# A transformer block on one core: one more iota at the end of GpSimd's queue

## The chip, the cores and the metric

The kernel runs on one core of a Trainium2 chip. Its time is the device time of one execution in microseconds (us). A time given for a kernel is the median of several runs. Executions of the same program follow each other on the core.

## The reference

The input x has 2048 rows of 512 numbers in bf16. It is layer-normalised to xn, and three things are added: x itself, an attention block on xn (32 heads of 16 columns each, softmax over all 2048 keys, output projection) and a gated feed-forward block on xn (inner width 1792). Cut to what matters:

```python
def _A_ref(x, wqkv, wo):
    qkv = (x @ wqkv).reshape(B, S, 3, H, Dh)  # then q, k, v by head
    scores = jnp.einsum("bhqd,bhkd->bhqk", q, k) * (Dh ** -0.5)
    p = _softmax(scores, axis=-1)
    o = jnp.einsum("bhqk,bhkd->bhqd", p, v)
    return o.transpose(0, 2, 1, 3).reshape(B, S, D) @ wo

def _B_ref(x, W_gate, W_up, W_down):
    gate = jnp.einsum("bsd,df->bsf", x, W_gate)
    up = jnp.einsum("bsd,df->bsf", x, W_up)
    gate = gate * (gate > 0)
    return jnp.einsum("bsf,fd->bsd", gate * up, W_down)

xn = _layernorm(x, axis=-1)
return x + _A_ref(xn, A_wqkv, A_wo) + _B_ref(xn, B_W_gate, B_W_up, B_W_down)
```

## The kernel before

**The order of the work.** The program is written as a list of operations (`G.op(engine, duration, function, ...)`). A planner in the class `Graph` places them on five queues by dependence, priority and the durations that it is given, and works out the waits between the queues. Each queue then runs strictly in order on its engine: an instruction that waits holds up all that stand behind it on that engine.

**The start.** Four tiles of x (128 rows each) are fetched first (line 723, on SP's queue), then the first columns of Wq and Wk (lines 736 and 737), four more tiles of x, Wv, and the last eight tiles of x, which go to the buffer `hT`. TensorE runs ten matmuls on zeros (`heat`, line 1021) whose result nobody uses. Each of the first tiles is normalised by itself: VectorE takes its mean and variance (lines 810 and 812), for tile 3 ScalarE takes them (lines 801 and 802); VectorE adds the small constant (`vare`, lines 792 and 804); GpSimd raises to the power of -0.5 (`rstd`, lines 794 and 808); VectorE applies it (`xn_sb`, line 833). TensorE transposes the tile (line 858), ScalarE copies it out of PSUM (`xnT`, line 866), and TensorE projects the first keys and queries from it (line 1039). ScalarE and VectorE write the queries of four heads apart, each multiplied with a column of `hmask` that is not zero in the rows of its head alone (lines 1064 and 1065).

**Where the mask comes from.** `hmask` is made from the number of the partition. GpSimd writes that number into `pid`, two columns of the buffer `ints`, with an iota (line 687). It is the first operation of the kernel on GpSimd's queue. VectorE masks it (line 688, `ints`) and compares it four times (line 691, `hmask`). These five instructions stand on VectorE's queue ahead of the first statistics of line 810.

**The long middle.** Scores of 128 keys by 512 queries are made on TensorE (line 138 is the helper that records nearly all matmuls). Most are exponentiated on ScalarE (line 1525, 708 times). For the rest VectorE makes three shifted integer patterns that together stand for the exponential: line 1481 the first, and for most of these the second and third are made by GpSimd with a 64-bit integer addition (line 1495, 308 times). Between these TensorE works off the projections and the feed-forward block as fillers.

**GpSimd's libraries.** The names of the program tell two kinds of operations on GpSimd: those called `stock` (the powers) and the 64-bit addition. `load_library` (line 883) places one 64-bit addition of two words at line 886, ordered behind all operations called `stock`, and gives the planner 7000 ns (`LIB_NS`) for it. The compiler puts a pair of instructions `MODIFY_POOL_CONFIG` on GpSimd's queue wherever the next operation is of the other kind, and ahead of the first one of the program: so a pair stands in front of the iota of line 687 and one in front of the addition of line 886. The last operation on GpSimd's queue is an addition of line 1495.

**The end.** Behind the last scores, VectorE and TensorE normalise and project the last heads (`normalise_last`, lines 1272 to 1298), and four tiles of the result are stored, the last by ScalarE's queue (line 1305). At line 584 all queues meet.

Of the kernel before, what the change touches and what calls it, by code (L numbers as in the profile page):

```python
# [83 lines left out]
LIB_NS = 7000  # L84
# [521 lines left out]
def bass_parallel_sum__mha_block__glu_gated_reglu__prompt_kernel(  # L606
# [13 lines left out]
    with ExitStack() as es:  # L620
        def sb(name, shape, dt):
# [4 lines left out]
        pid, word = ints[:, 0:2], ints[:, 2:4]  # L626
# [36 lines left out]
        G = Graph()  # L663
# [17 lines left out]
        t_id, t_pid, t_expo, t_warm, t_zero = (Tile() for _ in range(5))  # L681
        t_masks = [Tile() for _ in range(4)]
# [6 lines left out]
             reads=[t_pid], writes=[t_pid], prio=-890)  # L689
        for v in (0, 2, 1, 3):  # L690
            G.op("DVE", 100, lambda e, v=v: e.tensor_scalar(hmask[:, v:v + 1], pid[:, 0:1], 16.0 * v, QSCALE, op0=ALU.is_equal, op1=ALU.mult),
                 reads=[t_pid], writes=[t_masks[v]], prio=-889 + v)
# [3 lines left out]
                                                    base=0, pattern=[[-1, 128]], channel_multiplier=1),  # L696
             reads=[t_id], writes=[t_id], prio=-898)
        t_rbz = Tile()
# [70 lines left out]
        for j in range(4):  # L769
            for ee in range(2):  # L770
                r0 = 32 * j + DH * ee
                dma(lambda e, r0=r0, ee=ee: e.dma_start(Wo_l[r0:r0 + DH, ee, :], A_wo[D - 128 + r0:D - 128 + r0 + DH, :]), 16,
                    reads=[t_woz], writes=[Tile()], prio=60, after=100)
# [230 lines left out]
        NU = len(units)  # L1004
# [52 lines left out]
        for v in (0, 2, 1, 3):  # L1057
# [3 lines left out]
            for n, (tile, bank, c, x) in enumerate(((pb, 3, slice(0, 384), slice(0, 384)), (bq, 1, slice(128, 256), slice(384, 512)))):  # L1061
# [4 lines left out]
                     reads=[tile, t_masks[v]], writes=[] if n else [t1], joins=[q0], prio=MASK_LATE + v if late else -787 + 0.2 * v + 0.1 * n,  # L1066
# [446 lines left out]
        for u, unit in enumerate(units):  # L1513
# [8 lines left out]
            for sub in range(2):  # L1522
# [3 lines left out]
                              reads=[ts], writes=[tr], prio=u - 100, order=[exp_ops[u - 1]] if u else [], name="ex%d" % u)  # L1526
# [7 lines left out]

        assert li == len(plan)

        normalise_last(*last_pv)

        def blank_early(e):
# [38 lines left out]
```

## Time and profile before

| what | value |
|---|---|
| time, median of 3 runs | 692.18 us (691.84 to 692.42) |
| time of the profiled execution | 691.33 us |
| its span, first to last instruction | 689.4 us |
| TensorE busy (matmuls) | 673.2 us, 98% of the span |
| ScalarE busy | 659.8 us, 96% |
| VectorE busy | 588.5 us, 85% |
| GpSimd busy | 330.0 us, 48% |
| mean granted TensorE clock | 0.992 |

PE is TensorE's matmuls, PEld its weight loads, DVE VectorE, ACT ScalarE, POOL GpSimd, SP the queue that issues most DMAs. A name with a q behind it (POOLq, SPq) is the sequencer of that engine: instructions that compute nothing. In a row of the timeline stand the start, the time taken, the engine, the line, the operation with its output and input, and in square brackets how long the engine had been idle and what ended that. The chain that ended last is followed back from the last instruction, at each step to what released it. "issue" is time in which the engine waited for nothing that the profile shows. A row of the windows gives, for a stretch of time, the busy time of each engine with the number of its instructions, the granted TensorE clock (1.00 is full speed) and the busy share of the DMA engines.

### The profile page before, as it was taken

Reading aid. Unit: us, or ns where it says so; the run is one execution under the profiler, and the core shown is the slowest. Engines: PE = TensorE matmul, PEld = TensorE weight load, DVE = VectorE, ACT = ScalarE, POOL = GpSimd, SP = SyncE. Lnnn points to the kernel's source line nnn. Section 1 sums busy time; section 2 is a strip of 40 time slices with the busy share of each in tenths; the row PEclk is TensorE's granted clock in tenths of the full one; section 3 lists DMA queues with packets and bytes.
Section 4 is the critical chain, followed back from the end, with each engine's and each line's share of the span. In section 5 each row is a group of like instructions: output and inputs, shape, how many; then the busy total and the mean of one; then the engine's idle time right before and its main releaser. Section 6 shows DMA issues by size and latency. Waiting matters only on the chain.

```text
span 689.4 us, 46060 instructions
## 1 busy us (share of the span) xinstructions
PE 673.2 (98%) x22320; PEld 399.4 (58%) x20890; DVE 588.5 (85%) x993; ACT 659.8 (96%) x725; POOL 330.0 (48%) x340
## 2 busy tenths in 40 slices
PE   5899999999999999999999999999999999999997
PEld 2455665566655556656565556555655667655574
DVE  5975897999989878889899787889999887998876
ACT  3999999999999999999999999999999999999984
POOL 2311334445455546545455564445566654555540
PEclk7999999999999999999999999999999999999999
DMA  6330010231311111110101121110100121120001
GB/s 190 60 70 27 21 44 12 53 93 36 92 42 27 44 49 38 31 41 11 45 6 28 32 50 47 30 42 16 39 5 18 39 69 41 42 58 13 20 13 34
DMA packets 51478, 28.77 MB, mean 42 GB/s; under 512 B 18840, under 2 KB 50328, under 8 KB 51288
## 3 DMA queue, kind: packets, MB, share of 16 engines
q1 hardware_dynamic: 51144, 25.70, 14.4%
q8 instruction: 169, 2.77, 1.8%
q14 instruction: 21, 0.17, 0.1%
q10 hardware_dynamic: 144, 0.13, 0.1%
HBM read 18.22 MB, written 2.10 MB: 29 GB/s over the span
## 4 chain that ended last, share of the span: by engine, by line
PE 82%; ACT 12%; DVE 4%; issue 2%; POOL 0%; DVEq 0%; POOLq 0%
PE ps L138 81%; ACT ring L1525 12%; DVE stats L810 1%; DVE qd L1481 1%; PE ps L1039 1%; PE ps L858 0%; DVE qd L1498 0%; DVE xn_sb L1298 0%; POOL rstd L794 0%; DVE v_aug L978 0%; DVE kT L971 0%; DVE xnT L878 0%; DVE ints L688 0%; DVE qT L1065 0%; DVE up_sb L1277 0%
## 5 line engine op out<-in xcount | busy, mean ns | idle before, releaser
L1525 ACT ACTIVATE ring<-ps 128x1024 bf16<-128x1024 f32 x708 | 651.7, 1115 | 8.2 <-PE ps L138 8.1
L138 PE MATMUL ps<-qT,kT 64*32 64x512 bf16 x8192 | 463.8, 375 | 1.7 <-issue 0.6
L1495 POOL INT64_ADD qd<-qd x308 | 317.2, 1040 | 309.5 <-DVE qd L1481 176.7
L1481 DVE TENSOR_SCALAR qd<-ps 128x512 int16<-128x512 f32 x632 | 413.3, 685 | 59.4 <-PE ps L138 53.1
L138 PE MATMUL ps<-qd,v_aug 64*32 64x512 bf16 x3792 | 301.4, 375 | 0.2
L138 PE MATMUL ps<-ring,v_aug 64*32 64x512 bf16 x2832 | 241.9, 375 | 0.6 <-issue 0.5
L1461 PEld LDWEIGHTS <-kT 64*32 64x32 bf16 x8132 | 175.1, 92 | 110.9 <-issue 25.1
L1433 PEld LDWEIGHTS <-v_aug 64*32 64x32 bf16 x5252 | 128.2, 92 | 64.1 <-issue 11.2
L138 PE MATMUL ps<-xnT,wgs 64*32 64x512 bf16 x1792 | 137.5, 375 | 0.0
L138 PE MATMUL ps<-xnT,wus 64*32 64x512 bf16 x1792 | 135.8, 375 | 0.0
L138 PE MATMUL ps<-Wd,hT 64*32 64x512 bf16 x768 | 58.4, 375 | 0.2 <-issue 0.2
L913 PEld LDWEIGHTS <-wgs 64*32 64x32 bf16 x1792 | 43.8, 92 | 23.4 <-issue 4.1
L913 PEld LDWEIGHTS <-hT 64*32 64x32 bf16 x1792 | 43.7, 92 | 22.6 <-issue 2.4
L913 PEld LDWEIGHTS <-wus 64*32 64x32 bf16 x1792 | 44.5, 92 | 21.2 <-issue 2.7
L1130 DVE COPY up_sb<-ps 128x512 f32<-128x512 f32 x56 | 38.4, 685 | 7.4 <-PE ps L138 7.3
L1134 DVE SCALAR_TENSOR_TENSOR hT<-ps,up_sb 128x512 bf16<-128x512 f32 x56 | 38.3, 684 | 2.7 <-PE ps L138 2.6
L138 PE MATMUL ps<-Wv,hT 64*32 64x512 bf16 x512 | 39.4, 375 | 0.2 <-issue 0.2
L138 PE MATMUL ps<-Wk,hT 64*32 64x512 bf16 x512 | 39.2, 376 | 0.0
L138 PE MATMUL ps<-Wo_p,x_sb 64*32 64x512 bf16 x480 | 37.1, 376 | 0.1
L138 PE MATMUL ps<-xnT,Wq 64*32 64x512 bf16 x480 | 37.2, 375 | 0.0
L138 PE MATMUL ps<-xnT,Wk 64*32 64x512 bf16 x480 | 36.1, 375 | 0.7 <-issue 0.4
L138 PE MATMUL ps<-Wv,xnT 64*32 64x512 bf16 x512 | 30.7, 375 | 0.3
(82 smaller groups left out, 224.8 us busy)
## 6 DMA issues: line engine op xcount, KB each, us to landing
wus<-in_B_W_up_dram SPq DMA_DIRECT2D x38, 128.0 KB, 2.4
wgs<-in_B_W_gate_dram SPq DMA_DIRECT2D x38, 128.0 KB, 2.5
xr_sb<-in_A_x_dram SPq DMA_DIRECT2D x16, 128.0 KB, 2.5
qT<-qf SPq DMA_DIRECT2D x120, 16.0 KB, 2.4
o_sb<-o_sb SPq DMA_DIRECT2D x60, 32.0 KB, 2.5
out_dram<-xn_sb SPq DMA_DIRECT2D x15, 128.0 KB, 1.9
x_sb<-in_A_x_dram SPq DMA_DIRECT2D x8, 128.0 KB, 2.9
Wd<-in_B_W_down_dram SPq DMA_DIRECT2D x6, 128.0 KB, 2.6
```

The lines of the kernel that those rows point to most:

```text
L138: return e.add_instruction(mybir.InstMatmult(name=e.bass.get_next_instruction_name(), engine=mybir.EngineType.PE, ins=[e.lower_ap(x), e.lo ...
L810: G.op("DVE", 580, lambda e, m=m: e.bn_stats(stats[:, m, :], xs(m)), reads=[t_xm[m]], writes=[t_st], prio=pr, order=last_xn if m == 4 and ...
L913: e.ldweights(w()[rows, 32 * j:32 * j + 32], tile_position=(rows.start, 32 * j))
L1039: ins = e.matmul(ps[32 * j:32 * j + 32, BANK[bank], c], w[:, dt, 32 * j:32 * j + 32], xnT[:, dt, x], start=(dt == 0), stop=(dt == DT - 1), ...
L1130: G.op("DVE", 603, lambda e: e.tensor_copy(up_sb[:, tup.slot, :], bank_of(tu)), reads=[tu], writes=[tup], prio=-590)
L1134: G.op("DVE", 603, lambda e: e.scalar_tensor_tensor(out=hT[:, th.slot, :], in0=bank_of(tg), scalar=0.0, in1=up_sb[:, tup.slot, :], op0=ALU ...
L1433: e.ldweights(vs(j), tile_position=(64 * half, 32 * j))
L1461: e.ldweights(ks(m), tile_position=(64 * half, 32 * m))
L1481: G.op("DVE", 601, lambda e, j=j, tx=tx: e.tensor_scalar(qd[:, tq.slot, 512 * j:512 * j + 512], ps[:, BANK[tx.slot], :], IBIAS[3], 0.0, op ...
L1495: G.op("POOL", POOL_NS, lambda e, x=x, n=n: e.int64_add(x().bitcast(I64), raw().bitcast(I64), SHIFTS[n + 1] * LANES), reads=[ti, tq, t_lib ...
L1525: exp_ops[u] = G.op("ACT", 904, lambda e, tr=tr, k0=k0: e.activation(ring[:, tr.slot, :, :], ps[:, 4 * k0:4 * k0 + 2, :], ACTF.Exp, scale= ...
```

## The change

Behind the last addition of line 1495, one more iota is placed on GpSimd's queue. It writes the number of the partition into `pid` again, as line 687 does. Nothing reads it. `order` holds it behind all operations named `p3`, which are the additions of line 1495, and behind the two memsets of `rb`. It has no semaphore to signal. As it is an operation of the first kind behind one of the second, the compiler puts a pair of `MODIFY_POOL_CONFIG` in front of it. As built, GpSimd's queue is longer by these instructions at its end, and every other queue has the same instructions in the same order as before.

```diff
         assert li == len(plan)
 
+        added = [o for o in G.ops if o.name == "p3"]
+        G.op("POOL", LIB_NS, lambda e: e.iota(pid, pattern=[[0, 2]], base=0, channel_multiplier=1), reads=t_masks, writes=[t_pid], prio=NU, order=added + t_rbz.w, name="stock")
+
         normalise_last(*last_pv)
```

## The prediction

> **What bounds the kernel now.** I read the page first (engines, chain), then the chain of the first 20 us in order of time, then the rows around the two places where GpSimd changes its kind of operation, and last the end of GpSimd's queue.
>
> ```profile
> span 689.4 us, 46060 instructions
> PE 673.2 (98%) x22320; PEld 399.4 (58%) x20890; DVE 588.5 (85%) x993; ACT 659.8 (96%) x725; POOL 330.0 (48%) x340
> PE 82%; ACT 12%; DVE 4%; issue 2%; POOL 0%; DVEq 0%; POOLq 0%
> 60.00:100.00 40.00, 39.78 (x1356) 25.87 (x1308) 32.64 (x53) 39.72 (x45) 13.25 (x13) 1.00 0.13 32
> ```
>
> The middle is TensorE with ScalarE close behind: from 60 to 100 us they are busy 39.78 and 39.72 of 40 us (first two engines after the length are PE and PEld, then DVE, ACT, POOL). No wait is left there to shorten. So whatever shifts the start of this stage shifts the end by the same amount, and the change touches only GpSimd's end and, if anything, GpSimd's start.
>
> The chain of the start, from the view of the chain in order of time (start, length, what):
>
> ```profile
> 0.81 0.01 POOLq L687
> 0.82 0.02 issue
> 0.85 0.01 POOLq L687
> 0.86 7.24 issue
> 8.10 0.14 POOL ints L687
> 8.24 0.02 issue
> 8.26 1.17 DVE ints L688
> 9.44 0.02 issue
> 9.46 0.34 DVE hmask L691 x4
> 9.80 0.61 DVE stats L810
> ```
>
> The chain runs through 7.24 us in which GpSimd does nothing that is recorded, between the pair in front of the iota and the iota. VectorE's line 688 waits for the iota, and the first statistics stand behind it.
>
> ```profile
> L687 POOLq MODIFY_POOL_CONFIG  x2: 11/11/11, 0.8 to 0.8; - x2
> L886 POOLq MODIFY_POOL_CONFIG  x2: 11/11/11, 34.6 to 34.6; - x2
> 40.72 0.18 POOL L886 INT64_ADD ints<-ints  x1 [6.32 <-issue]
> 34.40:40.72 6.32, 6.22 (x200) 4.00 (x192) 6.32 (x14) 6.32 (x8) 0.00 (x0) 1.00 0.36 80
> 669.67 1.04 POOL L1495 INT64_ADD qd<-qd  x1 [0.46 <-PE ps L138]
> 670.71:689.40 18.69, 15.20 (x458) 9.07 (x398) 13.23 (x27) 8.83 (x12) 0.00 (x0) 0.97 0.10 32
> ```
>
> The same gap follows the second pair: 6.1 us from 34.6 to 40.72. So the pair itself takes 11 ns twice, and the first operation of the new kind comes 6 to 7 us later: code is exchanged. The second exchange costs nobody anything: in its window PE, DVE and ACT are busy (6.22, 6.32, 6.32 of 6.32 us; I read the columns as above). The last addition of line 1495 ends at 670.71. From there GpSimd is empty for 18.69 us.
>
> What is known of the exchange is also in the Trainium skill (GPSIMD Engine Reference, section 2.1 Instruction dispatch): `ModifyPoolConfig` loads code, and the first call to a freshly loaded kernel pays about 6 us with no visible instruction. The 7.24 and 6.1 us here agree.
>
> **The change, part by part.** *The tail.* It adds a pair, an exchange and an iota behind 670.71. By the rows of the two exchanges this takes 6.1 to 7.24 us, plus 0.14 us for the iota: done at 677.0 to 678.1, some 11 us ahead of the end. What hides it is the 18.69 us of the last window; without that cover it would cost its whole length. No instruction stands behind it on GpSimd but the meeting of all queues at line 584, and nobody waits for `pid`. In the exchange at 34.6 no engine lost time, so I put the tail at 0.
>
> *The start.* I take it that executions follow each other with nothing of GpSimd's between them. Then an execution of before begins with the code of the 64-bit addition in place, since an addition was the last thing that GpSimd did. The pair of line 687 then really exchanges code. An execution of after begins with the code that the iota needs already there. What a pair costs that asks for code already in place, no row shows. It is bounded below by its own two records, 0.02 us, and above by 7.24 us. I take the lower end: each of the gaps in the trace stands where the kind does change, the 308 additions behind line 886 run one after another without such a gap, and the length of the gap fits moving code, which is not needed then.
>
> What the start is then bound by, from the timeline and the tile's view:
>
> ```profile
> 0.74 1.82 SPq L723 DMA_DIRECT2D x_sb<-in_A_x_dram  x4
> DMA to landing us min/median/max: 2.2/2.9/3.5
> 4.78 0.63 ACT L801 ACTIVATE up_sb<-x_sb 128x512 bf16<-128x512 bf16 x1 [2.54 <-DMA x_sb<-in_A_x_dram]
> 6.17 0.19 ACT L802 ACTIVATION_READ_ACCUMULATOR up_sb<-x_sb,warm 128x1 f32 x1
> 9.71 0.68 DVE L810 BATCH_NORM_STATS2 stats<-x_sb 128x6 f32<-128x512 bf16 x1
> 13.03 0.15 DVE L804 TENSOR_SCALAR vare<-warm 128x1 f32<-128x1 f32 x1
> 3.08 0.51 SPq L737 DMA_DIRECT2D Wk<-in_A_wqkv_dram  x1
> Wk<-in_A_wqkv_dram SPq DMA_DIRECT2D x1, 128.0 KB, 3.8
> 14.23 0.62 PE L1039 MATMUL ps<-xnT,Wk 128*32 128x128 bf16 x16
> ```
>
> The iota comes at about 0.9, ends at 1.0; line 688 takes 1.17, line 691 0.34: VectorE is free at 2.6. The first statistics need tile 0 of x. Issued at 0.74 and landing 2.2 to 3.5 later, it is there between 2.9 and 4.2. ScalarE starts on the fourth tile at 4.78 when its DMA lands, the issues are 1.82/4 = 0.46 apart, so tile 0 is there at about 4.78 - 3 x 0.46 = 3.4; I take 3.5. The statistics move from 9.71 to 3.5: **6.2 us**. They are late next for the DMA, no more for the iota, and a pair that cost up to 0.9 us would still be hidden. The others follow: the constant for tile 3 (line 804) moves from 13.03 to 6.8 and needs line 802, done at 6.36; Wk is there at 3.08 + 3.8 = 6.9 and wanted at 14.23 - 6.2 = 8.0. So this term is 5.5 (tile 0 at 4.2) to 6.7 (line 804 on line 802).
>
> *TensorE's clock at the start.* A second gain hangs on the first.
>
> ```profile
> 5.43 0.40 PE L1540 MATMUL ps<-Wo_l 128*128 128x512 bf16 x1
> 12.56 1.74 PE L858 MATMUL ps<-ident,xn_sb 128*128 128x128 bf16 x12 [6.73 <-DVE vare L792]
> 8.50:9.00 0.50, 0.00 (x0) 0.87 0.81 260
> 12.56:18.12 5.56, 5.55 (x79) 0.50 0.27 87
> 19.00:19.20 0.20, 0.20 (x12) 0.73 0.00 0
> 13.20 1.73 ACT L866 ACTIVATE xnT<-ps 128x512 bf16<-128x512 bf16 x3 [6.85 <-PE ps L858]
> 18.80 2.85 ACT L1525 ACTIVATE ring<-ps 128x1024 bf16<-128x1024 f32 x3 [0.39 <-PE ps L138]
> 19.21 0.56 DVE L1079 CAST kT<-ps 128x384 bf16<-128x384 f32 x1 [1.25 <-PE ps L1039]
> ```
>
> The matmuls on zeros end at 5.83. TensorE then stands idle for 6.73 us, the clock falls to half at 8.87 (the window to 9.00 has 0.87), 3.0 us into the idle time, and stays there to 19.1, so that the first transposes and projections, 5.55 us busy, run at half speed. With the first transposes at 12.56 - 6.2 = 6.4 the idle time is 0.5 us. I take it that the clock then does not fall. At full speed 5.55 becomes 2.8 us. Not all of that is gained, as ScalarE's copies of line 866 and VectorE's work lie between: VectorE's one idle stretch there, 1.25 us at line 1079, waits for TensorE and would go. I take **1.2 us**, with 0 (the clock stays at half) and 1.4 us (half of TensorE's 2.8 us, the rest behind ScalarE) as ends. The Trainium skill (TensorE: Matmul & The Clock Gate, Part 1) says that the clock falls after an idle window of about 3.4 us; the 3.0 us here agree within the window's phase, and by that rule too an idle time of 0.5 us leaves the clock as it is.
>
> *What could take it back.* Later loads have room:
>
> ```profile
> 6.08 1.53 SPq L723 DMA_DIRECT2D hT<-in_A_x_dram  x3
> hT<-in_A_x_dram SPq DMA_DIRECT2D x2, 256.0 KB, 5.9
> 22.03 0.69 DVE L810 BATCH_NORM_STATS2 stats<-hT 128x6 f32<-128x512 bf16 x1
> ```
>
> The ninth tile of x is there at 6.08 + 5.9 = 12.0, wanted at 22.03 - 7.4 = 14.6. Everything that SP issues behind 20 us waits for other engines and moves with them.
>
> **The sum.** 691.33 (the profiled execution, span 689.4 and 1.93 around it) - 6.2 - 1.2 + 0 = 683.9 us. The median is 0.85 above that execution (692.18), so for the median 684.8 us. The ends are 692.18 - 8.1 = 684.1 and 692.18 - 5.5 = 686.7. I widen them by 1.3 us on either side: below because a shift of this start may let other small waits before 28 us go, above because the pair may cost some of its 7.24 us also with the code in place (a pair of 3.5 us would bring VectorE to line 810 at 0.86 + 3.5 + 0.14 + 1.17 + 0.34 = 6.0 and leave 3.7 us and half of the clock's term).
>
> **The rivals.** *The pair always loads.* If the pair fetches the code whether or not it is there, the start stays as it is, 0.86 to 8.10, and the tail is hidden: 692.2 us, no change. For it speaks that the program asks for the load with the same instructions in each case, and that no row shows a shorter one; against it only that the trace's loads all do change the code. It would come out the same if something between two executions put other code in place. By the Trainium skill's rule (GPSIMD Engine Reference, section 2.1) that the first call to a freshly loaded kernel pays, it would come out so if a repeated request counts as a fresh load. No row of before can tell.
>
> *The pair costs a part.* Between the two, some 4 to 6 us of the 7.24 remain: VectorE reaches line 810 at 0.86 + 4 + 1.65 = 6.5 to 8.5, a gain of 3.2 to 1.2 us: about 690 us. For it speaks that two instructions are issued, of which one may drop the old code and the other fetch the new; against it that their own records are 11 ns each.
>
> *The tail is seen.* Slower, if the exchange at the end took longer than the 18.69 us from 670.71 to the end: GpSimd would then be the last at line 584. At 20 us it would give 692.2 + 1.3 = 693.5, with no gain at the start. Against it: the two exchanges measured take 6.1 and 7.24 us, the shorter with the DMA engines busy 0.36 of the time, and in the last window they are busy 0.10.
>
> **How the numbers follow.** The forecast (code in place, load skipped) has 0.82, the part 0.05, the load that always runs 0.10, the seen tail 0.03. Differences under 0.2% (1.4 us) can't be told from none here. Faster by more: 0.82 and the part, 0.87. Same 0.10, slower 0.03. The range of the forecast, 682.8 to 688.0, holds nearly all of its 0.82, which leaves out no more than 2 in 10.
>
> **What the profile of after would show.** If right: the iota of line 687 at about 1 us with "issue" before it nearly gone, the first row of line 810 at 3.4 to 4.2 released by a DMA of x, a granted clock that stays up from 6 us on, line 1525 starting near 11.4 in place of 18.80, and at the end an iota at 677 to 678 with nobody waiting. If wrong: the iota of line 687 still at 8.1, or, for the tail, a chain whose last piece is on GpSimd. The second term fails by itself if the first transposes come at 6.4 but windows up to 12 us show 0.50.

## The result and the profile after

| | before | after |
|---|---|---|
| time, median | 692.25 us (4 runs, 691.84 to 692.42) | 683.12 us (4 runs, 681.67 to 683.50) |
| time of the profiled execution | 691.33 us | 682.77 us |
| span | 689.4 us | 680.6 us |
| mean granted TensorE clock | 0.992 | 1.000 |

The ratio is 0.9865 (95% interval 0.9848 to 0.9882): 9.1 us faster. The forecast was 684.8 us with a range of 682.8 to 688.0.

The start of the changed kernel, first by the instructions of line 687 and then by the timeline:

```profile
L687 POOLq MODIFY_POOL_CONFIG  x2: 11/11/11, 1.0 to 1.0; - x2
L687 POOL IOTA ints<- x1: 129/129/129, 1.1 to 1.1; 128x2 int32 x1
```

```profile
1.07 0.13 POOL L687 IOTA ints<- 128x2 int32 x1 [0.64 <-POOLq L1566]
1.23 0.17 DVE L688 TENSOR_SCALAR ints<-ints 128x2 int32<-128x2 int32 x1
1.44 0.34 DVE L691 TENSOR_SCALAR hmask<-ints 128x1 f32<-128x1 int32 x4
2.88 0.69 DVE L810 BATCH_NORM_STATS2 stats<-x_sb 128x6 f32<-128x512 bf16 x1 [1.11 <-DMA x_sb<-in_A_x_dram]
5.84 1.43 PE L858 MATMUL ps<-ident,xn_sb 128*128 128x128 bf16 x12
6.22 0.14 DVE L804 TENSOR_SCALAR vare<-warm 128x1 f32<-128x1 f32 x1
7.96 1.17 PE L1039 MATMUL ps<-xnT,Wq 128*32 128x384 bf16 x32
10.29 3.07 ACT L1525 ACTIVATE ring<-ps 128x1024 bf16<-128x1024 f32 x3
```

The pair is still there and its two records are as long as before, 11 ns each. But the iota follows it at once, at 1.07 us where it stood at 8.10. The mask is ready before the first tile of x, and VectorE's first statistics now wait for the DMA (the square brackets of the fourth row), as forecast. They begin at 2.88 in place of 9.71. ScalarE's first exponential stands at 10.29 in place of 18.80.

The end, by GpSimd's timeline and the windows (after the length: PE, PEld, DVE, ACT, POOL busy, granted clock, DMA share, GB/s):

```profile
660.85 1.04 POOL L1495 INT64_ADD qd<-qd  x1 [0.46 <-PE ps L138]
668.95 0.13 POOL L1538 IOTA ints<- 128x2 int32 x1 [7.05 <-issue]
```

```profile
5.86:12.00 6.14, 5.06 (x109) 2.63 (x107) 5.85 (x22) 5.51 (x12) 2.71 (x5) 1.00 0.94 286
661.89:680.60 18.71, 15.25 (x458) 8.21 (x398) 13.23 (x27) 8.83 (x12) 0.13 (x2) 1.00 0.10 33
```

The exchange at the end takes 7.05 us and lies beside 18.7 us of other work: VectorE and ScalarE are busy in the last window for as long as they were before (13.23 and 8.83 us). TensorE's clock, 0.50 between 9 and 19 us before, is 1.00 in the first of the two windows, and the 32 projections of the queries (line 1039 with Wq) take 1.17 us. Before, the timeline had for them:

```profile
15.32 1.90 PE L1039 MATMUL ps<-xnT,Wq 128*32 128x384 bf16 x32
```

Where do the 9.1 us come from? The first of the 15 rows of VectorE's line 955 serves as a mark: it stands where the start is over and the steady middle begins. Before and after:

```profile
42.91 0.69 DVE L955 TENSOR_SCALAR qf<-ps 128x512 bf16<-128x512 f32 x1 [0.31 <-PE ps L138]
```

```profile
34.62 0.69 DVE L955 TENSOR_SCALAR qf<-ps 128x512 bf16<-128x512 f32 x1 [0.32 <-PE ps L138]
```

The mark is 8.29 us earlier. From the mark to the end the two profiled executions take 646.5 and 646.0 us. So all of the gain that can be placed lies in the start. The half microsecond behind the mark is not explained by the change: in two more profiled executions of the changed kernel, further down, the same stretch took 649.4 and 644.1 us.

### The profile page after: what moved, and what is told of

The parts are those of the page before. It is cut to its first block, busy times and chain, and to the rows that moved or that the text cites. A ratio compares the mean times of both kernels' runs of the same rounds, so it can differ in the third digit from the quotient of the medians.

```text
span 680.6 us, 46065 instructions
## 1 busy us (share of the span) xinstructions
PE 671.9 (99%) x22322; PEld 397.0 (58%) x20890; DVE 587.0 (86%) x993; ACT 659.8 (97%) x725; POOL 330.8 (49%) x341
## 3 DMA queue, kind: packets, MB, share of 16 engines
q8 instruction: 169, 2.77, 1.7%
## 4 chain that ended last, share of the span: by engine, by line
PE 85%; ACT 10%; DVE 4%; issue 0%; DMA 0%; POOL 0%; DVEq 0%
PE ps L138 85%; ACT ring L1525 10%; DVE stats L810 1%; DMA x_sb<-in_A_x_dram 0%; DVE qd L1481 0%; DVE xn_sb L833 0%; DVE qd L1498 0%; DVE mv L812 0%; DVE xn_sb L1298 0%; POOL rstd L794 0%; DVE v_aug L978 0%; DVE kT L971 0%; DVE xnT L878 0%; DVE qT L1065 0%; DVE up_sb L1277 0%
```

## The experiments

They ran in three groups, each on one chip, and each is compared with the kernel before in its own group, whose median was 688.41 us in the first, 692.63 in the second and 687.66 in the third. Absolute times are not compared across groups. The mark (first row of line 955) stood at 34.62, 34.67 and 34.65 us in three profiled executions of the changed kernel, on different occasions, and carries the finer readings.

**A memset in the iota's place.** It computes on GpSimd as well, but needs no exchange, so no pair stands before it.

```diff
-        G.op("POOL", LIB_NS, lambda e: e.iota(pid, pattern=[[0, 2]], base=0, channel_multiplier=1), reads=t_masks, ...
+        G.op("POOL", 100, lambda e: e.memset(pid, 0), reads=t_masks, ...
```

> The changed kernel with a memset of pid in the iota's place. A memset needs no exchange of code, so no pair stands in front of it. Theory (the time depends on which code GpSimd holds when an execution begins): the 64-bit addition's code is left in place, the iota of line 687 comes at 8.1 us as before, 692.2 us. Rival (any further instruction behind the last addition does it): 683.1 us.

Measured: 688.47 us against 688.41, ratio 0.9998 (0.9988 to 1.0008). No gain. The iota of line 687 is back at 7.88 us:

```profile
0.85 7.03 issue
7.88 0.14 POOL ints L687
```

(The chain in order of time.) A further instruction at the end is not what does it.

**Both exchanges at the end.** One 64-bit addition behind the new iota, so that the last code in place is the addition's.

```diff
         G.op("POOL", LIB_NS, lambda e: e.iota(pid, ...), ..., name="stock")
+        G.op("POOL", LIB_NS, lambda e: e.int64_add(word.bitcast(I64), word.bitcast(I64), 0), reads=[t_word], writes=[t_word], prio=NU, order=G.ops[-1:])
```

> The changed kernel with one 64-bit addition of the two words behind the new iota, so that a second pair and a second exchange follow at the end and the addition's code is the last. Theory: the tail takes some 7 + 6 = 13 us, still hidden, but line 687 pays its 7.2 us again: 692.2 us. Rival (the iota or the exchange at the end does it, whatever is left in place): 683.1 us.

Measured: 688.09 us against 688.41, ratio 0.9997 (0.9985 to 1.0008). GpSimd's timeline of the end and of the start:

```profile
667.37 1.04 POOL L1495 INT64_ADD qd<-qd  x1 [0.46 <-PE ps L138]
675.45 0.13 POOL L1538 IOTA ints<- 128x2 int32 x1 [7.04 <-issue]
681.55 0.18 POOL L1539 INT64_ADD ints<-ints  x1 [5.98 <-issue]
```

```profile
8.60 0.13 POOL L687 IOTA ints<- 128x2 int32 x1 [8.18 <-issue]
```

The new iota is there with its exchange, and a second exchange of 5.98 us behind it, both hidden. The start pays again. So neither the iota nor its exchange is worth anything by itself; what counts is the code that an execution leaves in place for the next. This shows at the same time that the code stays in place from one execution to the next. What a first execution finds, behind another program, was not run.

**The clock without the iota.** The kernel before with more matmuls on zeros.

```diff
-            for _ in range(10):
+            for _ in range(38):
```

> The kernel before with 38 in place of 10 matmuls on zeros in line 1021, so that TensorE works until about 12 us and its clock does not fall; the iota still comes at 8.1 us. This is the clock's part alone. Theory: the clock's part is 1.2 to 1.8 us: 690.4 to 691.0 us, the first row of line 810 still at 9.7 us. Rival (the clock gives nothing, and all 9.1 us come from the earlier iota): 692.2 us.

Measured: 687.48 us against 688.41, ratio 0.9982 (0.9971 to 0.9993), by the interval 0.5 to 2.0 us faster. The iota and the statistics stand as in the run with the memset (7.89 and 9.51 us here; 7.88 and 9.50 there). TensorE's clock stays up: the first 12 transposes take 1.41 us, where they took 1.74 before and 1.43 in the changed kernel. The mark moves from 42.30 (the run with the memset) to 41.23, so by 1.07 us:

```profile
41.23 0.69 DVE L955 TENSOR_SCALAR qf<-ps 128x512 bf16<-128x512 f32 x1 [0.32 <-PE ps L138]
```

```profile
42.30 0.69 DVE L955 TENSOR_SCALAR qf<-ps 128x512 bf16<-128x512 f32 x1 [0.32 <-PE ps L138]
```

The first fence is the run with 38 matmuls, the second that with the memset. Against the run with the memset, the clock is worth 1.07 us by itself; against the kernel before it is more, as the section on the prediction shows.

**The iota without the clock.** The changed kernel with a single matmul on zeros.

```diff
-            for _ in range(10):
+            for _ in range(1):
```

> The changed kernel with 1 in place of 10 matmuls on zeros in line 1021: the earlier iota without the warm clock. Theory: the statistics still begin at 2.9 us, the clock is at half for the first projections, and the 1.2 to 1.8 us are lost: 684.3 to 684.9 us. Rival (the clock gives nothing): 683.1 us.

Measured: 681.41 us, ratio to before 0.9897 (0.9874 to 0.9920), 7.0 us faster. The changed kernel was not timed in this group; where it was, its ratios were 0.9865, 0.9896 and 0.9893, with intervals that overlap this one, so the times cannot separate the two. The mark can:

```profile
35.78 0.69 DVE L955 TENSOR_SCALAR qf<-ps 128x512 bf16<-128x512 f32 x1 [0.31 <-PE ps L138]
```

It is 1.16 us later than in the changed kernel's 34.62, in line with the 1.07 us of the run before. The chain shows what is slow:

```profile
6.43 1.11 PE ps L858 x8
7.54 0.55 PE ps L1039 x16
8.09 0.54 PE ps L858 x4
8.63 2.79 PE ps L1039 x43
```

These lengths are those of the kernel before at half clock, whose chain has for the last of these rows:

```profile
15.39 2.79 PE ps L1039 x44
```

The column of the granted clock shows 1.00 in all windows of this run up to 14 us, which the lengths contradict. Where the column and the lengths differ, I go by the lengths (the last section says where the column misleads).

**VectorE's queue alone.** The kernel before with the five instructions of the mask moved behind the statistics of tiles 0 to 2.

```diff
         G.run()
+        q = G.queue["DVE"]
+        masks = [o for o in q if -890 <= o.prio <= -886]
+        third = [o for o in q if o.dur == 580][2]
+        q[:] = [o for o in q if o not in masks]
+        put = q.index(third) + 3
+        q[put:put] = masks
```

> The kernel before with VectorE's five instructions for the mask (lines 688 and 691) moved behind the statistics of tiles 0 to 2 on its queue. Nothing else moves. Theory: the statistics begin at 2.9 us, but the powers of line 794 stand behind the iota on GpSimd and still come at 9.7 us in place of 11.33: 1.7 us faster than before, and the clock still falls. Rival (holding up VectorE's queue was the whole cost of the late iota): 6 us or more faster.

Measured: 691.09 us against 692.63, ratio 0.9972 (0.9957 to 0.9988): 1.5 us between the medians, 0.8 to 3.0 us by the interval. From VectorE's and GpSimd's timeline and the chain:

```profile
2.77 0.69 DVE L810 BATCH_NORM_STATS2 stats<-x_sb 128x6 f32<-128x512 bf16 x1 [1.63 <-DMA x_sb<-in_A_x_dram]
8.19 1.16 DVE L688 TENSOR_SCALAR ints<-ints 128x2 int32<-128x2 int32 x1 [2.50 <-POOL ints L687]
10.18 0.41 DVE L833 TENSOR_SCALAR xn_sb<-x_sb,mv,rstd 128x512 bf16<-128x512 bf16 x1 [0.46 <-POOL rstd L794]
```

```profile
8.03 0.13 POOL ints L687
9.28 0.28 POOL ident L695
9.56 0.59 POOL rstd L794
```

The statistics run at 2.77, but the first power comes at 9.56 all the same, behind the exchange and GpSimd's other work. It is 1.77 us earlier than before (11.33), as expected. The mark stands at 40.26, 2.65 us earlier than before, as the clock also came back sooner (at 15.4 us in place of 19.1). Of the 8.29 us, freeing VectorE's queue alone recovers these 2.65; the other 5.6 were held by GpSimd's own queue.

**Requests for code in place.** The changed kernel with a request for the addition's code in front of ten additions.

```diff
+                    again = n == 0 and nq[0] % 15 == 0
-                    G.op("POOL", POOL_NS, lambda e, x=x, n=n: e.int64_add(...),
+                    G.op("POOL", POOL_NS, lambda e, x=x, n=n, again=again: (e.load_library(library_config.all_libraries[1]) if again else None, e.int64_add(...))[1],
```

> The changed kernel with a further request for the code of the 64-bit addition in front of about ten of the additions of line 1495, while that code is in place. Theory (a request for code in place costs next to nothing): no gap of more than 0.1 us behind any of them that the waits don't explain, time of the changed kernel within 1 us. Rival (only the first request of an execution is skipped): 6 us of GpSimd's time at each, which its idle time hides only in part; later additions are late, several us slower.

Measured: 685.21 us; the changed kernel in the same group 685.25 (its expectation below). The instructions of the line of the additions:

```profile
L1496 POOLq MODIFY_POOL_CONFIG  x20: 11/11/11, 121.2 to 635.5; - x20
L1496 POOL INT64_ADD qd<-qd x308: 1033/1038/1062, 56.9 to 662.5; - x154
...
  issue: 0.2, 1
```

Ten more pairs, and GpSimd's idle time that nothing else explains is 0.2 us in all. One exchange would have been 6. Nor did a wait hide one: in the trace each of the ten additions begins 0.07 to 0.08 us behind its pair. This was the price that no row of before showed: a request for code in place is close to nothing, here at the start and at ten places between 121 and 636 us.

> The changed kernel once more, timed beside the runs below. Theory: 8.3 to 9.3 us under the kernel before; by the starts of one row of TensorE in the traces so far (45.80 us before, 37.50 us after) 8.3 us.

Measured: 685.25 us against 692.63, ratio 0.9896 (0.9880 to 0.9912), 7.4 us faster; mark at 34.67. The expectation of 8.3 to 9.3 was missed; only the upper end of the interval, 8.3 us, reaches it. The start is as early as in the first trace, so the difference lies behind the mark, where this execution took 649.4 us.

**The end without cover.** Two attempts. In the first the new iota waits for VectorE's last instruction:

```diff
+        for o in [o for o in G.ops if o.eng == "DVE"][-1:]:
+            G.ops[-1].deps[o] = True
```

> The changed kernel with the new iota held until VectorE's last instruction (line 1298) is done, so that the exchange of code at the end has nothing beside it. Theory: VectorE ends at 677.4 us of the changed kernel's 680.6; the pair, some 7.05 us and the iota of 0.13 follow: the end comes at 684.7, 4.1 us later than in the changed kernel, and the start stays early. Rival (the exchange runs behind the end of an execution at no cost): same as the changed kernel.

Measured: 683.72 us, ratio to before 0.9880 (0.9855 to 0.9906), the same as the changed kernel in this group (685.25, ratio 0.9896). The instructions of the new line, and GpSimd's timeline:

```profile
L1542 POOLq MODIFY_POOL_CONFIG  x2: 11/11/11, 662.9 to 663.0; - x2
```

```profile
679.09 0.14 POOL L1542 IOTA ints<- 128x2 int32 x1 [16.15 <-DVE xn_sb L1298]
```

The run did not test what it was meant to. The wait belongs to the iota, the pair stands ahead of it, and the exchange began at 663.0 while the iota waited: the iota starts at 679.09, 0.09 us behind the end of VectorE's last instruction at 679.00, with no 7 us between. So an exchange starts when the queue reaches the pair, and hides behind a wait of the instruction that needs it. For the second attempt a memset, which needs no exchange, takes the wait, and the pair and the iota stand behind it:

```diff
+        G.op("POOL", 100, lambda e: e.memset(pid, 0), reads=t_masks, writes=[t_pid], prio=NU, order=added + t_rbz.w)
+        for o in ends:
+            G.ops[-1].deps[o] = True
+        G.op("POOL", LIB_NS, lambda e: e.iota(pid, ...), writes=[t_pid], prio=NU, name="stock")
```

> The changed kernel with a memset of pid, which needs no exchange, waiting for VectorE's last instruction (line 1298), and the pair and the iota behind it. Now the pair itself is held, where in the run before only the iota was. Theory: the exchange has nothing beside it; 6.8 to 7.5 us and the iota follow VectorE's end, which is 3.2 us ahead of the span's end, so the end comes some 4.1 us later than in the changed kernel. Rival (the exchange costs nothing at the end even so): same as the changed kernel.

> The changed kernel, timed beside the held pair on the same chip. Theory: 7 to 9 us under the kernel before, by the trace's start 8.3 us.

Measured: 685.68 us (ratio 0.9970, 0.9959 to 0.9980) with the pair held, 680.70 (0.9893, 0.9872 to 0.9914) for the changed kernel beside it, 687.66 for the kernel before. The changed kernel's 7.0 us are at the lower end of what was expected (7 to 9). Held, the exchange costs 5.0 us of the 7.0 us gained. From the instructions of line 584, where the queues meet, and GpSimd's timeline, of the run with the pair held:

```profile
L584 SPq DRAIN  x1: 13/13/13, 677.8 to 677.8; - x1
L584 POOLq EVENT_SEMAPHORE  x2: 17/17/17, 682.8 to 682.9; - x2
```

```profile
675.44 0.10 POOL L1542 MEMSET ints<- 128x2 int32 x1 [16.12 <-DVE xn_sb L1298]
682.54 0.13 POOL L1545 IOTA ints<- 128x2 int32 x1 [6.99 <-issue]
```

SP, otherwise the last, is done at 677.8; GpSimd comes 5.0 us later. That is the price of the tail without the cover that it has in the changed kernel. It was expected at 4.1 us, and most of the difference comes from a misreading: the expectation put VectorE's end at 677.4 us in the changed kernel, but the three rows of line 1298 end at 678.0, 2.6 us ahead of the span's end in place of 3.2.

## Why the prediction was right, step by step

*The mechanism* was right: the program's last use of GpSimd decides which code the next execution finds, and a request for code in place does not load it. The prediction could only assume both. The run with both exchanges shows the first, the ten requests show the second, and the trace of after shows the two together. Of the rivals, the pair that always loads and the pair that costs a part fall with the iota at 1.07 us; the tail that is seen falls with the iota at 668.95, 11.7 us ahead of the end. The lower end chosen for the unknown price, 0.02 us, was the right one: the iota follows the second record of the pair within 0.1 us. It was a choice: as the prediction says, no row of before could decide it.

*The tail at 0* was right: its length was forecast at 6.1 to 7.24 us plus the iota, measured 7.05 plus 0.13. The run with the pair held puts the cost without cover at 5.0 us.

*The first term* was 6.2 us for the statistics (5.5 to 6.7), measured 6.83 (9.71 to 2.88), just above its own upper end. The step that was off is the arrival of tile 0, taken at 3.5 us from the spacing of the issues; it was there at 2.88, slightly below the lowest end that I gave (2.9). VectorE was free even earlier than I worked out, at 1.8, not 2.6, since line 688 took 0.17 us in place of 1.17. The bound by line 802 did not hold either: ScalarE started on tile 3 at 4.47 in place of 4.78, and line 804 moved by 6.81 us.

*The second term*, the clock, was 1.2 us (0 to 1.4). Its mechanism was right, and it hangs on the first as said: without the earlier iota the transposes meet a clock that has fallen. Its size depends on when the clock comes back. The traces record the moments at which the granted clock changes, and the windows of 0.2 us around them show it; for the run with the memset and for the run with both exchanges:

```profile
17.60:17.80 0.20, 0.20 (x8) 0.55 0.29 82
```

```profile
16.20:16.40 0.20, 0.20 (x8) 0.53 0.00 0
```

| profiled run (us) | first statistics | clock back at full | mark | statistics to mark |
|---|---|---|---|---|
| before | 9.71 | 19.11 | 42.91 | 33.20 |
| changed, one matmul on zeros | 2.93 | 11.39 | 35.78 | 32.85 |
| memset in the iota's place | 9.50 | 17.78 | 42.30 | 32.80 |
| both exchanges | 10.22 | 16.39 | 42.27 | 32.05 |
| before, 38 matmuls on zeros | 9.51 | does not fall | 41.23 | 31.72 |
| changed | 2.88 | does not fall | 34.62 | 31.74 |

In the last two rows the clock stays up, and the way from the statistics to the mark is 31.72 and 31.74 us, though the statistics begin 6.6 us apart. In the other four it is the longer, the longer the clock stays down behind the statistics (9.4, 8.5, 8.3 and 6.2 us). So the clock's part is 1.07 us against the run with the memset and 1.11 against the run with one matmul, but 1.46 us against the kernel before (33.20 - 31.74), just above the upper end of 1.4. Luck enters here: the clock's changes follow each other by 3.41, 6.83 or 10.24 us in the start of these traces, once, twice or three times the same step, and where the steps fall differs from run to run. What sets that was not tried.

The changed kernel leaves no idle time there, as its transposes follow the matmuls on zeros directly; in the run with the pair held TensorE stood idle for 0.57 us, and the projections still took 1.17. The rule of the Trainium skill (TensorE: Matmul & The Clock Gate, Part 1), by which so short an idle time leaves the clock as it is, agrees with that. The idle time ahead of a fall is no fixed number here: it was 2.4 us in the run with the memset, 2.9 with VectorE's queue changed, 3.0 before and 3.5 with both exchanges. The first is well under the 3.4 us that the prediction takes from the Trainium skill, and the measurement decides.

*The sum.* 7.4 us were forecast, and the mark moved by 8.29: 6.83 of the first term and 1.46 of the second. Both came out just above their upper ends, and together above the sum's own end of 8.1. That the range holds the result is owed to the 1.3 us by which it was widened, and these were meant for other small waits. From the mark's 8.29 to the 9.1 of the medians: the profiled executions differ by 0.5 more behind the mark and by 0.2 less in what lies around the span (8.56 us in all), and the medians stand 0.92 us above the profiled execution before and 0.35 after, which makes the other 0.6. The three comparisons gave 9.1, 7.4 and 7.0 us (ratios of 0.9865, 0.9896 and 0.9893); the middle of the kernel varies from execution to execution by more than that remainder, and nothing here ties it to the change.

## What to carry to other kernels

Look at the first instruction on GpSimd that stands behind a pair of `MODIFY_POOL_CONFIG`, and at what ended the idle time before it: 6 to 8 us of "issue" there was an exchange of code in these runs, and if it lies in the start of a kernel that is run again and again, ask which code the execution before left in place. Ending with the code that the start needs moves the exchange to the end, where here 18.7 us without use of GpSimd cover it; without such cover 5.0 of the 7.0 us go back. Put the pair early and the wait behind it, as the exchange runs while the next instruction waits, and count what stands behind the late instruction on its own queue as well as on the queue that waits for it.

## What the runs showed that I had not expected

The exchange is started by the queue reaching the pair, not by the instruction that needs the code being ready: in the run with the waiting iota it was done while the iota waited 16.15 us.

The exchange has two lengths. From the pair to the next instruction it took 5.6 to 6.1 us where the code of the 64-bit addition came in, and 6.7 to 7.8 us where the other code did, over all runs.

VectorE's line 688, a 128x2 integer operation, takes 1.16 to 1.17 us in the traces where it starts at 8.05 to 8.77, and 0.17 us in the changed kernel, where it starts at 1.23. GpSimd's long memset of line 706 starts 0.11 us behind it in the changed kernel and 0.13 to 0.14 in the others, so that alone does not tell them apart. The cause was not tried.

The column of the granted clock showed full speed in a run whose matmuls took the lengths of half speed (2.79 us for the projections of line 1039). The trace of that run settles why: its first record of the clock is the rise to full speed at 11.39 us, and ahead of a first record the column shows 1.00 without a measurement. The same holds for the first microseconds of the kernel before: its first record is a rise at 5.46 us, and the matmuls on zeros, 128x512 each, take 0.61 to 0.63 us ahead of it and 0.40 us at it.
